# A layer of spectral mixing and expert retrieval on one core: fold sums and turned tiles by DMA, half the tiles negated, small statistics on GpSimd, zero products

## The chip, the cores and the metric

The kernel runs on one core of a Trainium2 chip. The core has a matrix engine (TensorE, PE in the profile, with its weight loads as PEld), a vector engine (VectorE, DVE), an engine for activations (ScalarE, ACT), a general engine (GpSimd, POOL) and a queue engine that mainly starts transfers (SyncE, SP). Each works through its own list of instructions in order, and waits for the others through semaphores. The metric is the time of one execution on the device in microseconds (us); less is better.

## What is computed

The input x has 2048 rows of 512. Its layernorm feeds two branches, whose results are added to x.

```python
a = einsum("bsd,ed->bse", x, dft_hid_re); b = einsum("bsd,ed->bse", x, dft_hid_im)
y = einsum("ts,bse->bte", dft_seq_re, a) - einsum("ts,bse->bte", dft_seq_im, b)
# second branch, 32 heads, 64 x 64 experts
q = einsum("bsd,dhk->bshk", x, w_q)            # halves q1, q2 of 128 each
s1 = q1 . k1, s2 = q2 . k2                     # 64 scores each
# the two best of each, combined, softmax, then rows of u and v:
out = sum over chosen (gate * gelu(x . u[row])) * v[row]
```

The first branch is the real part of a two-dimensional discrete Fourier transform. The second scores each row against two small sets of keys for every head, keeps the best pairs, and mixes rows of two tables.

## The kernel before

The 2048 rows are held as 16 tiles of 128 x 512, in four groups g, each of four tiles q; group order is G = (1, 0, 2, 3). `xn[g]` is a group's tile of 128 x 4 x 512 (x_raw in the profile for group 1, xq for the others). The work has a front, from the start to the first score, and a long rest: the scores (s, line 962; twelve products of 512 columns for each tile and block of heads), interleaved with the products m of the next block, and after them the products with the tables (z, g, v). This change is all in the front. What the front does, group by group:

- **Statistics and norms** (`ln_a`, `ln_b`): BN_STATS and its aggregate for each tile on DVE, a root on ACT, a reciprocal on DVE (line 353) and four small operations (356 to 359), which make `rstd` and `negm`. Then ACT normalises the four tiles in place (371). Where small scratch for BN_STATS is needed, it is taken from the fold's or the statistics' own tiles. A single row, `x5`, is normalised apart (376) and written into group 0's tile later (651).
- **Folds** (`fold_t`, `fold_d`, `fold`): for the first factor (k = 0) the sum of tiles 0, 1 and tiles 2, 3 (407), for the second (k = 1) their difference, 128 x 1024 each, both on DVE; then sums and differences of mirrored columns, with a copy of four columns on GpSimd (399), up to the operand zq (425, 426; v for the last two groups of k = 1).
- **First and second factor** (`main`, 446): for each k and group four f32 products of 512 columns, summed over the groups in four banks of PSUM, p. The row's two products stand apart (`main_row`, 450). `evict` copies the banks out.
- **m** (145, `m_mul`): products of the key matrix with the query weights, which give m, against which tiles are scored. The weights are loaded in four pieces, wq0_0 to wq0_3; the next block's, wq1, are loaded later (131), split into two f16 parts on ACT and GpSimd (155, 160, 163) and used in the m products between scores (141).
- **Turned tiles**: the scores need each tile turned, as two f16 parts (`xt`). For groups 1 and 0 PE turns them (`xpose`: `xpose_a`, 506, four products of a tile with the identity; ACT evicts the upper part, 509; `xpose_b`, 517, subtracts it with `idn`; ACT evicts the lower part, 519). For groups 2 and 3 ACT casts (`upper`, 532), DVE makes the rest (`lower`, 535), and an SP transfer turns both (`cross`, 539).

The program is written in the order of the code; a scheduler then orders each engine's list by its own costs, within dependencies and explicit orders: `pace(i, x)` and `behind(i, x)` put instruction i after x, and `on_dve` returns the DVE instructions of a piece of code. Transfers are queued on the engine that starts them, in its list.

## Time and profile before

| | us |
|---|---|
| median of 3 runs | 1072.82 |
| lowest and highest | 1071.03, 1073.52 |
| profiled execution | 1075.39 |
| its span in the trace | 1073.5 |
| PE busy in the span | 1056.6 |
| DVE busy | 939.7 |
| ACT busy | 732.5 |
| POOL busy | 635.9 |

The span is the time from the first to the last instruction in the trace. A busy share of 98% for PE is an average over all stages; what bounds a stage is read from its waits and its timeline. The clock that PE was granted is part of the page as a row of tenths, one for each fortieth of the span, and of the view by windows with two decimals. The lines that carry the argument are shown with the prediction.

### The profile page before, as it was taken

The page shows a single profiled execution, that of the slowest core. Times are in us where ns is not written, and L with a number is a line of the kernel's source. Part 1 is how long each engine was busy: PE and PEld are TensorE (multiplying, and loading weights), DVE is VectorE, ACT ScalarE, POOL GpSimd, SP SyncE. Part 2 cuts the span into 40 slices and gives each one's busy share as a digit, 9 for nine tenths or more (in the row PEclk, how much of TensorE's full clock was granted, in tenths as well). Part 3 has the DMA queues.
Part 4 walks back from the last instruction along what each step waited for, and adds up shares of the span by engine and source line. Part 5 has one row for each costly group of instructions (what it writes and reads, how often), then busy time and mean ns, then how long its engine had stood idle before and what let it go on. Part 6 is the DMA issues. An engine that isn't in the chain of part 4 may idle for free.

```text
span 1073.5 us, 28588 instructions
## 1 busy us (share of the span) xinstructions
PE 1056.6 (98%) x11101; PEld 698.0 (65%) x11101; DVE 939.7 (88%) x2683; ACT 732.5 (68%) x1367; POOL 635.9 (59%) x610
## 2 busy tenths in 40 slices
PE   6999999999999999999999999999999999999998
PEld 4444555444444544986876958768586785967867
DVE  7979686888999999988999888998999889989972
ACT  5886667859879677435777668676676775868641
POOL 1154858688888755035666566665477757566520
PEclk9899999999999999999999999999999999999999
DMA  9176466345536331377867677776778867676521
GB/s 357 67 193 201 147 242 204 122 151 179 182 137 217 103 120 66 92 256 218 238 191 228 187 233 215 218 219 213 218 205 239 251 190 217 214 237 192 151 50 53
DMA packets 96500, 198.86 MB, mean 185 GB/s; under 512 B 23744, under 2 KB 39381, under 8 KB 96358
## 3 DMA queue, kind: packets, MB, share of 16 engines
q1 hardware_dynamic: 75160, 124.87, 35.7%
q0 software_dynamic: 20896, 71.84, 23.1%
q8 instruction: 88, 1.44, 0.6%
q14 instruction: 54, 0.44, 0.1%
q10 hardware_dynamic: 302, 0.27, 0.1%
HBM read 176.66 MB, written 17.10 MB: 180 GB/s over the span
## 4 chain that ended last, share of the span: by engine, by line
PE 92%; DVE 3%; POOL 2%; issue 1%; DMA 0%; ACT 0%; SPq 0%; POOLq 0%; ACTq 0%
PE z L1138 28%; PE s L962 27%; PE v L1206 26%; PE g L1175 4%; PE p L446 3%; PE m L141 1%; PE vl L1206 1%; DVE vals L970 1%; POOL u L764 1%; DVE idx L974 1%; DMA x_raw<-in_x_dram 0%; PE hy L546 0%; PE hy L545 0%; POOL cx L918 0%; PE xp L506 0%
## 5 line engine op out<-in xcount | busy, mean ns | idle before, releaser
L962 PE MATMUL s<-m,xq 128*128 128x512 f16 x1536 | 338.1, 379 | 0.7 <-ACT ss L967 0.7
L1138 PE MATMUL z<-xb,u 128*128 128x128 f16 x5376 | 306.8, 219 | 0.0
L1138 PEld LDWEIGHTS <-u 128*128 128x128 f16 x5376 | 301.4, 98 | 2.8
L1206 PE MATMUL v<-v,act 128*128 128x512 f16 (+1 forms) x1344 | 288.1, 373 | 0.0
L1270 POOL TENSOR_TENSOR ov<-ov,ga 128x512 f32<-128x512 f32 x125 | 174.0, 1392 | 173.4 <-ACT ga L1262 116.4
L962 PEld LDWEIGHTS <-xq 128*128 128x128 f16 x1536 | 148.2, 98 | 173.9 <-issue 1.8
L1206 PEld LDWEIGHTS <-act 128*128 128x128 f16 x1440 | 138.6, 98 | 141.5 <-issue 2.2
L1233 POOL DMA_INDIRECT ga<-in_uv_dram,eix x128 | 164.9, 1289 | 41.3 <-POOL ov L1270 36.4
L1162 DVE TENSOR_TENSOR L<-io_lam,cmp 128x2048 f16<-128x2048 f16 x112 | 156.9, 1414 | 34.0 <-PE g L1175 29.4
L970 DVE MAX8 vals<-ss 128x8 f32<-128x64 f32 x1024 | 152.7, 216 | 25.3 <-ACT ss L967 25.3
L1141 ACT ACTIVATE act<-z,scl 128x512 f32<-128x512 f32 x112 | 76.2, 681 | 76.5 <-PE z L1138 69.1
L974 DVE FIND_INDEX8 idx<-vals,ss 128x8 uint16<-128x256 f32 x256 | 107.2, 419 | 0.0
L967 ACT ACTIVATE ss<-s,wsc 128x512 f32<-128x512 f32 x112 | 75.3, 683 | 44.2 <-PE s L962 28.4
L944 ACT ACTIVATE cx<-cx 128x896 f32<-128x896 f32 x64 | 60.5, 946 | 58.8 <-DVE cx L924 32.5
L1262 ACT ACTIVATE ga<-ga,za 128x512 f32<-128x512 f32 x128 | 92.2, 722 | 9.7 <-issue 0.2
L1191 ACT ACTIVATE act<-g 128x1024 f16<-128x1024 f32 x56 | 73.2, 1310 | 28.0 <-DVE g L1186 26.0
L1249 DVE SCALAR_TENSOR_TENSOR ga<-ga,px 128x512 f32<-128x512 f32 x128 | 85.9, 677 | 0.0
L1194 DVE TENSOR_TENSOR act<-g,act 128x1024 f16<-128x1024 f32 x56 | 73.0, 1304 | 11.5 <-ACT act L1191 11.1
L1186 DVE SCALAR_TENSOR_TENSOR g<-act,scl,g 128x1024 f32<-128x1024 f32 x56 | 71.5, 1279 | 4.4 <-ACT act L1141 2.8
L1175 PEld LDWEIGHTS <-L 128*128 128x128 f16 x1792 | 51.9, 96 | 8.5 <-issue 2.3
L163 POOL TENSOR_TENSOR wq<-wq,wh 128x1024 f16<-128x1024 f32 x26 | 55.4, 2134 | 2.6 <-ACT wq L160 2.1
L1175 PE MATMUL g<-R,L 128*128 128x32 f16 x1792 | 54.1, 176 | 1.9 <-issue 1.9
(308 smaller groups left out, 1312.9 us busy)
## 6 DMA issues: line engine op xcount, KB each, us to landing
cx<-in_cb_dram SPq DMA_DIRECT2D x50, 448.0 KB
wq<-in_wq_dram SPq DMA_DIRECT2D x32, 512.0 KB
fit<-in_wq_dram SPq DMA_DIRECT2D x28, 512.0 KB
uv<-in_ut_dram SPq DMA_DIRECT2D x16, 512.0 KB
uv<-in_vn_dram SPq DMA_DIRECT2D x16, 512.0 KB
cx<-in_cb_dram SPq DMA_DIRECT2D x28, 224.0 KB
xt_d<-xq SPq DMA_DIRECT2D x16, 256.0 KB
y<-y_d SPq DMA_DIRECT2D x14, 256.0 KB
```

The source lines that it names most:

```text
L962: mm = nc.tensor.matmul(ps, xt[i][:, l, kd, :], m[:, r, kd, :], start=(n == 0), stop=(n == 3 * KD - 1))
L970: nc.vector.max(vals[:, i, w, :, h], s[:, g, :])
L974: nc.vector.max_index(idx[:, i, w].rearrange("p k h -> p (k h)"), vals[:, i, w, 0:2].rearrange("p k h -> p (k h)"), s[:, w * HC:g + 1, :]. ...
L1138: mm = nc.tensor.matmul(p[:, cc * P:(cc + 1) * P], ug[:, l, c % 2, kd, :], xb[:, r, kd, :], start=(n == 0), stop=(n == 3 * KD - 1))
L1141: GL[mm.ins.name] = nc.scalar.activation(act[:, cg * 4:cg * 4 + 4, :].rearrange("p c n -> p (c n)"), p, AF.Gelu_apprx_tanh, scale=zsc)
L1162: nc.vector.tensor_tensor(L.rearrange("p t (l two) -> p t l two", two=2), io_lam.rearrange("p (l two) -> p l two", two=2).unsqueeze(1).to_ ...
L1175: i = nc.tensor.matmul(p[:, hf, t * NC:(t + 1) * NC], L[:, t, :], R[:, hf * 16 + t, :], start=True, stop=True)
L1206: mm = nc.tensor.matmul(pv[d.start // 256][:, d], w16[:, c, :, l], vg[:, r, c % 2, d], start=(c == 0 and k == 0), stop=(c == NC - 1 and k ...
L1233: nc.gpsimd.indirect_dma_start(out=t, out_offset=None, in_=uv, in_offset=bass.IndirectOffsetOnAxis(ap=eix[:, n].rearrange("p k h -> p (k h ...
L1249: nc.vector.scalar_tensor_tensor(t, t, 1.0, T["x"], op0=ALU.mult, op1=ALU.mult, accum_out=T["z", n][:, s:s + 1])
L1262: nc.scalar.activation(t, t, AF.Copy, scale=z)
L1270: T["a"] = nc.gpsimd.tensor_tensor(o, o, t, op=ALU.add)
```

## The change

All of it is in the front.

1. The tiles q = 2, 3 of every group are normalised with negated factors, so they hold the negated values. The first factor's fold becomes a difference, and what reads those tiles takes the sign into account (`sgn`, two identities `idn`). `nr` holds negm and rstd together, and `off0` takes the place of `not0` for group 0.
2. BN_STATS has its own scratch tile `stx`.
3. For groups 2 and 3 the small operations after the reciprocal go to GpSimd; so do the norms of the row x5 and its later write.
4. The second factor's fold sum is made by transfers: SP copies tiles 0, 1 of groups 0, 2, 3 to new tiles `fb` (512 KB each), and GpSimd's accumulating transfer adds tiles 2, 3 (512 KB). For group 1 the accumulation is in place.
5. Group 0's turned tiles go the way of those of groups 2 and 3, with the space of two weight tiles; the 20 products on PE and eight evictions on ACT go.
6. Zero products (`warm`): 29 before the first m products, 13 after them, and 6 into bank p0_00 before group 0's products.
7. Some orders: the row's products stand within group 3's; h = 1 comes first in the last group of k = 0 and the first of k = 1; three of the four absolute maxima of m come before group 3's norms.

The core of the diff:

```diff
-                st = (FF[0, G[0]][:, 0] if n == 1 else SM[n - 1])[:, 6 * (q % 2):6 * (q % 2) + 6]
+                st = stx[:, 6 * (q % 2):6 * (q % 2) + 6]
...
+        if n > 1:
+            nc.gpsimd.tensor_scalar(vp[:, n - 2, 0], mvs[:, g, :, 1], 1e-5, None, op0=ALU.add)
+            nc.gpsimd.tensor_scalar(vp[:, n - 2, 1], mvs[:, g, :, 0], -1.0, None, op0=ALU.mult)
...
+        end = i
+        nm = da.tile([P, 2, 2], F32, name=f"nm{g}")
+        if n < 2:
+            nc.vector.scalar_tensor_tensor(sm[:, 0], var, 1e-5, sm[:, 1], op0=ALU.add, op1=ALU.mult)
+            nc.vector.scalar_tensor_tensor(sm[:, 2], sm[:, 0], -0.5, sm[:, 1], op0=ALU.mult, op1=ALU.mult)
+            nc.vector.scalar_tensor_tensor(rstd[:, g], sm[:, 2], 1.5, sm[:, 1], op0=ALU.add, op1=ALU.mult)
+            if n == 0:
+                nc.vector.tensor_tensor(nm[:, 0], mvs[:, g, 2:4, 0], rstd[:, g, 2:4], op=ALU.mult)
+                end = nc.vector.tensor_scalar(nm[:, 1], rstd[:, g, 2:4], -1.0, None, op0=ALU.mult)
+            else:
+                nc.vector.scalar_tensor_tensor(negm[:, g], mvs[:, g, :, 0], -1.0, rstd[:, g], op0=ALU.mult, op1=ALU.mult)
+                end = nc.vector.tensor_scalar(nm, nr[:, g, :, 2:4], off0, None, op0=ALU.mult)
+        else:
+            v, m = vp[:, n - 2, 0], vp[:, n - 2, 1]
+            nc.gpsimd.tensor_tensor(sm[:, 0], v, sm[:, 1], op=ALU.mult)
+            nc.gpsimd.tensor_tensor(sm[:, 0], sm[:, 0], sm[:, 1], op=ALU.mult)
+            nc.gpsimd.tensor_scalar(sm[:, 2], sm[:, 0], -0.5, 1.5, op0=ALU.mult, op1=ALU.add)
+            nc.gpsimd.tensor_tensor(rstd[:, g], sm[:, 2], sm[:, 1], op=ALU.mult)
+            nc.gpsimd.tensor_tensor(negm[:, g], m, rstd[:, g], op=ALU.mult)
+            nc.gpsimd.tensor_scalar(nm, nr[:, g, :, 2:4], -1.0, None, op0=ALU.mult)
         for q in (0, 2, 1, 3):
             t = xn[g][:, q]
             b, r = negm[:, g, q:q + 1], rstd[:, g, q:q + 1]
-            if g == 0 and q > 1:
-                b, r = nm0[:, 0, q - 2:q - 1], nm0[:, 1, q - 2:q - 1]
...
-                LN[n] = nc.scalar.activation(x5[:, q], x5[:, q], AF.Identity, bias=negm[0:1, 0, q + 2:q + 3],
-                                             scale=rstd[0:1, 0, q + 2:q + 3])
+                nc.gpsimd.tensor_scalar(x5[:, q], x5[:, q], rstd[0:1, 0, q + 2:q + 3], negm[0:1, 0, q + 2:q + 3],
+                                        op0=ALU.mult, op1=ALU.add)
...
-        op = ALU.subtract if k else ALU.add
+        if k:
+            FF["t"] = FB[g]
+            return after
         t = FF["t"] = da.tile([P, 2, 512], F32, tag="ft", name=f"ft{k}_{g}", bufs=1)
-        i = nc.vector.tensor_tensor(t, xn[g][:, 0:2], xn[g][:, 2:4], op=op)
+        i = nc.vector.tensor_tensor(t, xn[g][:, 0:2], xn[g][:, 2:4], op=ALU.subtract)
...
+    def fold_add(g, after):
+        if g == G[0]:
+            t = FB[g] = xn[g][:, 0:2]
+        else:
+            t = FB[g] = da.tile([P, 2, 512], F32, name=f"fb{g}")
+            nc.sync.dma_start(t, xn[g][:, 0:2])
+        pace(nc.gpsimd.dma_start(t, xn[g][:, 2:4], accum_op=ALU.add), after)
...
-        for h in range(2):
+        for h in (1, 0) if g == G[-1 - 3 * k] else (0, 1):
             r = A[k, g][:, h * 512:(h + 1) * 512]
             l = Q[k][g][:, h ^ k]
             for dt in range(2):
-                nc.tensor.matmul(PP[k][dt][h], l[:, dt * P:(dt + 1) * P], r, start=first, stop=last)
-
-    def main_row():
-        for dt in range(2):
-            nc.tensor.matmul(PP[0][dt][0], s5[:, dt * P:(dt + 1) * P], c5r, start=False, stop=False)
+                if last and (k, h) == (0, 0):
+                    nc.tensor.matmul(PP[0][dt][0], s5[:, dt * P:(dt + 1) * P], c5r, start=False, stop=False)
+                i = nc.tensor.matmul(PP[k][dt][h], l[:, dt * P:(dt + 1) * P], r, start=first, stop=last)
+        return i
...
+    def sgn(i):
+        return -XS if i // 4 > 1 else XS
...
-        n = ORD.index(i) % 8
-        t = TS[i] = uf[4 + n // 2][:, n % 2 * 512:n % 2 * 512 + 512].bitcast(F16).rearrange("p (a d) -> p a d", a=2)
-        pace(nc.scalar.activation(t[:, 0], xn[i % 4][:, i // 4], AF.Copy, scale=XS), LN[3])
+        n = ORD.index(i) - 8
+        s = uf[4 + n // 2] if n >= 0 else MS[0, 0 if n < -2 else 2].rearrange("p h k -> p (h k)")
+        t = TS[i] = s[:, n % 2 * 512:n % 2 * 512 + 512].bitcast(F16).rearrange("p (a d) -> p a d", a=2)
+        pace(nc.scalar.activation(t[:, 0], xn[i % 4][:, i // 4], AF.Copy, scale=sgn(i)), LN[3])
...
+    def warm(n, p, alone, after=None):
+        for _ in range(n):
+            i = nc.tensor.matmul(p, wz[:, 0:P], wz[:, P:], start=alone, stop=alone, skip_group_check=not alone)
+            if after is not None:
+                pace(i, after)
+        return i
...
+    wb = pa("warm")
+    first = warm(29, wb, True)
     for t in range(2):
-        m_mul(0, t, (0, 1))
+        i = m_mul(0, t, range(KD))
+    warm(13, wb, True, i)
...
-                for q in (0, 1):
-                    xpose_a(4 * q + G[0], True, LN[2])
...
+            FF["p2"] = FF["p"]
+            for q in range(4):
+                hi = xpose_a(4 * q + G[0], True, LN[3])
+        if n == 3:
+            fold_row(0, FF["end"])
         main(0, g)
         if n == 0:
-            for t in range(2):
-                m_mul(0, t, (2, 3))
             for t in range(2, 4):
-                m_mul(0, t, range(KD))
+                i = m_mul(0, t, range(KD))
+            warm(6, PP[0][0][0], False, i)
+    fold_add(G[0], FF["p2"])
+    for g in G[1:]:
+        fold_add(g, FF["p"])
+    for q in range(4):
+        xpose_b(4 * q + G[0], True, LN[3])
+    made = nc.cur_bb.bb.instructions
+    first = len(made)
+    at = da.tile([P, 1], F32, name="at")
+    m_rest = m_scale(0, MR, at)
+    behind(next(i for i in made[first:] if i.engine == mybir.EngineType.Activation), hi)
...
+        if n:
+            fold(1, g)
+        if n == 1:
+            fold_row(1, FF["end"])
+            nc.gpsimd.tensor_scalar(xn[0][0:1, 2:4], x5, -1.0, None, op0=ALU.mult)
+            small = on_dve(m_rest)
+            behind(small[0], FF["end"])
+        if n == 2:
+            behind(FF["d"][0], small[0])
+            for i in small[1:]:
+                behind(i, FF["end"])
...
-            nc.scalar.activation(xn[0][0:1, 2:4], x5, AF.Copy)
...
         main(1, g)
-        if n == 1:
-            for i in ORD[4:8]:
-                xpose(i, True)
-    for i in ORD[8:12]:
+    for i in ORD[4:12]:
         lower(i, FF["m"])
+    for i in ORD[4:8]:
+        cross(i)
```

In DVE's list this is the place of group 0's statistics, in the front, after group 1's fold. `mvs` holds the statistics, `sm0` the small ones of group 0, `xq0` and `xq2` are the raw tiles of groups 0 and 2. Before:

```order
L345 BN_STATS fo0_1_235<-xq0_100 128x6 x2
L346 BN_AGGR mvs_76<-fo0_1_235 128x2 x2
L353 RECIPROCAL sm0_289<-sm0_289 128x4
L356 SCALAR_TENSOR_TENSOR sm0_289<-mvs_76,sm0_289 128x4
L357 SCALAR_TENSOR_TENSOR sm0_289<-sm0_289 128x4
L358 SCALAR_TENSOR_TENSOR rstd_77<-sm0_289 128x4
L359 SCALAR_TENSOR_TENSOR negm_78<-mvs_76,rstd_77 128x4
L362 TENSOR_SCALAR nm0_158<-rstd_77,not0_79 128x2
L361 TENSOR_SCALAR nm0_158<-negm_78,not0_79 128x2
L345 BN_STATS sm0_289<-xq2_102 128x6 x2
```

Group 0's chain from the reciprocal to its last small operation stands unbroken, and group 2's BN_STATS follow. In the same place of DVE's list, now:

```order
L449 TENSOR_TENSOR zq_139<-fo0_1_295 128x257
L350 BN_AGGR mvs_76<-stx_159 128x2
L349 BN_STATS stx_159<-xq2_101 128x6
L360 RECIPROCAL sm0_345<-sm0_345 128x4
L350 BN_AGGR mvs_76<-stx_159 128x2
L366 SCALAR_TENSOR_TENSOR sm0_345<-mvs_76,sm0_345 128x4
L349 BN_STATS stx_159<-xq2_101 128x6
L367 SCALAR_TENSOR_TENSOR sm0_345<-sm0_345 128x4
L350 BN_AGGR mvs_76<-stx_159 128x2
L368 SCALAR_TENSOR_TENSOR nr_77<-sm0_345 128x4
L349 BN_STATS stx_159<-xq2_101 128x6
L373 SCALAR_TENSOR_TENSOR nr_77<-mvs_76,nr_77 128x4
```

Group 2's BN_STATS have moved in between group 0's small operations; two of group 0's own (not shown) have moved up into group 1's fold.

In GpSimd's list, where before there was only a copy of four columns for each fold, the following stands from group 3's statistics (`sm3`) on; `fb` are the new tiles of the fold sums, `nr` and `nm3` what group 3's norms read:

```order
L377 TENSOR_TENSOR sm3_413<-vp_158,sm3_413 128x4
L378 TENSOR_TENSOR sm3_413<-sm3_413 128x4
L466 DMA x_raw_149<-x_raw_149 128x1024
L379 TENSOR_SCALAR sm3_413<-sm3_413 128x4
L380 TENSOR_TENSOR nr_77<-sm3_413 128x4
L381 TENSOR_TENSOR nr_77<-vp_158,nr_77 128x4
L382 TENSOR_SCALAR nm3_424<-nr_77 128x4
L419 COPY ff0_3_472<-ft0_3_470 128x4
L419 COPY r5_0_481<-r5_0_481 1x2
L466 DMA fb0_495<-xq0_99 128x1024
L466 DMA fb2_498<-xq2_101 128x1024
L466 DMA fb3_501<-xq3_102 128x1024
```

The accumulating transfer of group 1 is issued in the middle of group 3's small operations, and the other three follow the copy of the row's fold.

In SP's list, this is the place of the second block's weight loads (`wq1`) at the end of the front. Before:

```order
L131 DMA wq1_0_599<-in_wq_dram 128x1024
L131 DMA wq1_1_601<-in_wq_dram 128x1024
L131 DMA wq1_2_603<-in_wq_dram 128x1024
L131 DMA wq1_3_605<-in_wq_dram 128x1024
L539 DMA_TRANSPOSE xq2_102<-u4_117 128x8x128 x2
L539 DMA_TRANSPOSE xq2_102<-u5_118 128x8x128 x2
```

The four loads stand ahead of the first transposes, those of group 2. And now:

```order
L577 DMA_TRANSPOSE xq0_99<-wq0_0_167 128x8x128 x2
L577 DMA_TRANSPOSE xq0_99<-wq0_2_176 128x8x128 x2
L131 DMA wq1_0_648<-in_wq_dram 128x1024
L131 DMA wq1_1_650<-in_wq_dram 128x1024
L131 DMA wq1_2_652<-in_wq_dram 128x1024
L131 DMA wq1_3_654<-in_wq_dram 128x1024
L577 DMA_TRANSPOSE xq2_101<-u4_116 128x8x128 x2
L577 DMA_TRANSPOSE xq2_101<-u5_117 128x8x128 x2
```

Group 0's four transposes have come in ahead of the loads.

84 lines of the change are left out of this document (36 added, 48 removed).

## The prediction

> **What bounds the kernel now.** I read the chain of work that ended last, then the waits of PE, then PE's timeline over the first 62 us, then the same stretch window by window, then the other engines there.
>
> ```profile
> PE 92%; DVE 3%; POOL 2%; issue 1%; DMA 0%; ACT 0%; SPq 0%; POOLq 0%; ACTq 0%
> PE m L145 <- DMA wq<-in_wq_dram: 9.4, 1, 9.4
> PE g L1175 <- issue: 1.9, 4, 0.5
> PE p L446 <- DVE zq L425: 0.8, 1, 0.8
> PE s L962 <- ACT ss L967: 0.7, 1, 0.7
> ```
>
> PE carries 92% of the chain. After its first operands (9.4 us) it waits 0.8 us once in the front and then hardly at all. So what the change does to the time is how far it moves the first score (s, L962); that shift passes to the end almost one to one. The timeline (start, length, engine, line, operation, count) shows what stands before it:
>
> ```profile
> 9.40 7.09 PE L145 MATMUL m<-k_sb,wq 128*128 128x64 f32 x32 [9.40 <-DMA wq<-in_wq_dram]
> 16.28 5.05 PE L446 MATMUL p<-v,zq 128*128 128x512 f32 x8
> 21.16 3.68 PE L145 MATMUL m<-k_sb,wq 128*128 128x64 f32 x32
> 25.64 5.40 PE L446 MATMUL p<-v,zq 128*128 128x512 f32 x8 [0.80 <-DVE zq L425]
> 30.88 1.91 PE L506 MATMUL xp<-ident,x_raw 128*128 128x128 f32 x16
> 33.25 3.59 PE L446 MATMUL p<-v,zq 128*128 128x512 f32 x8
> 36.77 1.98 PE L450 MATMUL p<-u,u 1*128 1x512 f32 x4
> 39.16 5.40 PE L446 MATMUL p<-v,zq 128*128 128x512 f32 x8
> 44.50 5.32 PE L446 MATMUL p<-c,zq 128*128 128x512 f32 x12
> 49.66 1.15 PE L506 MATMUL xp<-ident,xq 128*128 128x128 f32 x9
> 60.84 13.11 PE L962 MATMUL s<-m,xq 128*128 128x512 f16 x60
> ```
>
> The first score starts at 60.84. A row group's four products (8 records) take 3.59 in one row and 5.40 in two others: the clock.
>
> ```profile
> 22.50:25.90 3.40, 2.60 (x22) 2.46 (x22) 3.25 (x13) 3.30 (x10) 0.71 (x1) 1.00 1.04 409
> 25.90:29.30 3.40, 3.40 (x5) 1.36 (x5) 3.26 (x8) 2.93 (x8) 0.00 (x0) 0.50 0.98 387
> 36.80:39.50 2.70, 2.70 (x8) 1.05 (x8) 2.60 (x8) 2.70 (x6) 0.64 (x1) 1.00 0.00 0
> 39.50:43.00 3.50, 3.50 (x5) 1.35 (x4) 3.47 (x9) 2.43 (x6) 0.00 (x0) 0.51 0.00 0
> ```
>
> (Window, then its length, busy time of PE, PEld, DVE, ACT and POOL, granted clock, DMA share, GB/s.) Twice the granted clock is 0.50 for 3.4 us, each time costing about 1.7 us: after a stretch of small products with gaps (2.60 of 3.40 busy), and after one of one-row and f16 products without a gap. The first m products also ran at half pace (7.09 against 3.68 for the same 32), behind waits of other engines.
>
> In 25.64 to 60.84 PE is the chain, but with no reserve: group 3's products start at 39.16, just when its operand comes.
>
> ```profile
> 18.74 0.81 ACT L371 ACTIVATE xq<-xq,negm,rstd 128x512 f32<-128x512 f32 x1 [1.03 <-DVE negm L359]
> 18.88 1.28 DVE L345 BATCH_NORM_STATS2 sm<-xq 128x6 f32<-128x512 f32 x2
> 23.57 0.17 DVE L353 RECIPROCAL sm<-sm 128x4 f32<-128x4 f32 x1
> 25.09 0.81 ACT L371 ACTIVATE xq<-xq,negm,rstd 128x512 f32<-128x512 f32 x1
> 28.78 2.04 ACT L587 ACTIVATE u<-m 128x512 f32<-128x512 f32 x4
> 32.88 2.92 ACT L371 ACTIVATE xq<-xq,negm,rstd 128x512 f32<-128x512 f32 x4
> 41.40 0.71 ACT L193 ACTIVATE m<-u,fo 128x512 f16<-128x512 f32 x1
> 35.83 1.23 DVE L407 TENSOR_TENSOR ft<-xq 128x1024 f32<-128x1024 f32 x1 [1.62 <-ACT xq L371]
> 38.68 0.43 DVE L425 TENSOR_TENSOR zq<-fo 128x257 f32<-128x257 f32 x1
> ```
>
> So a second chain runs through statistics, norms on ACT and folds on DVE: the norms of groups 0, 2 and 3 start at 18.74, 25.09 and 32.88, and group 3's fold waits for ACT. Whatever delays these norms reaches PE.
>
> **The change, part by part.** All times are of the profiled execution, 1075.39 us (span 1073.5 and 1.9 around it), which lies 2.6 above the median of 1072.82; I add the difference to the median.
>
> Zero products. One 128x512 f16 product is 13.11/60 = 0.22 us. The 29 and the 13 stand where PE waits anyway, if they lift the clock by 9.4 and 16.3. Then m takes 3.7 instead of 7.1, and group 1's products 3.45 instead of 5.05. This gains nothing by itself, since group 0's operand still comes from DVE. The six add 1.3: 16.9 + 3.45 + 3.68 + 1.3 = 25.3, before that operand. If the clock is not up, they end at 26.5 to 27.9 and their cover is gone, which costs 0 to 1.
>
> Statistics between the folds. In the new order DVE has two BN_STATS (0.64 each) and aggregates (some 0.15) within group 1's fold, and two more pairs between group 0's reciprocal and its last small statistic. Group 1's operand comes near 16.8; group 0's norms start at about 19.9 instead of 18.74, +1.1. What is saved (two pairs fewer after it) falls in DVE's wait for ACT. Group 0's operand: 26.7 instead of 25.64.
>
> Small statistics on GpSimd. The nearest rows:
>
> ```profile
> L837 POOL TENSOR_TENSOR c<-c,if 128x64 f32<-128x64 f32 x7 | 2.3, 326 | 0.1
> 37.09 0.69 DVE L390 TENSOR_TENSOR ff<-ft 128x508 f32<-128x508 f32 x1
> 37.19 0.64 POOL L399 COPY ff<-ft 128x4 f32<-128x4 f32 x1 [3.52 <-DVE ft L407]
> L1215 POOL DMA_DIRECT2D y<-in_x_dram x14 | 14.3, 1023 | 2.1 <-DVE ok L1422 2.0
> ```
>
> Five operations lead from reciprocal to norm. At the first row's size or a little below, 0.25, they take 1.25; if each waits for a DVE operation as the copy seems to (37.19 + 0.64 ends with 37.09 + 0.69), 5 x 0.67 = 3.4. Before, reciprocal to norm took 25.09 - 23.57 = 1.5. The bounds are therefore -0.3 and +1.9 for each of groups 2 and 3; I take 0.1, nearer to the free size, as DVE runs single-input statistics and short folds there. Group 2: reciprocal at 24.7 + 1.6 gives norms at 26.3 (+1.2, nearly all of it group 0's delay), fold from 29.3, operand 32.7. Group 3: reciprocal at 31.1; within the chain stands one accumulating DMA, whose issue takes 1.02. 31.1 + 1.6 + 1.0 = 33.7. ACT is busy until 33.9 anyway (26.3 + 2.92, a root of 0.3, the four copies' 2.04, and three absolute maxima of 0.71 and a short read each, which now stand ahead of these norms). Norms 33.9 instead of 32.88, four of them 2.92, fold 36.9, then 38.68 - 35.83 = 2.85 and the second half of the operand: 40.5.
>
> The Trainium skill's GPSIMD Engine Reference, section 1. Specifications, says GpSimd shares its SBUF interfaces with VectorE and contends with DVE instructions that have two SBUF inputs. The copy's row agrees; by that rule alone the two chains would each take the 3.4 of the upper bound, and the sum below would be 1.9 to 3.8 higher.
>
> Group 3 and the row products. PE is idle from about 36.3 but for four short products, so I charge one half-rate stretch at the place of the old one: from 40.6 to 43.0, 2.4 us at half rate lose 1.2. The one-row products (1.98) move from a place before 38.7 into group 3's, onto the path. 40.6 + 3.45 + 1.98 + 1.2 = 47.2, against 44.50. They wait for the row's fold, which DVE does after group 3's operand, mixed with the second factor's first fold: some 2.6, a little less than the 2.85 of a whole fold, so at 43.1. At half rate PE gets there at 43.5 and the wait is hidden; at full rate it gets there at 42.3 and waits 0.8.
>
> The Trainium skill, TensorE: Matmul & The Clock Gate, Part 1: The HAM clock gate, says that the rate is half or full by how busy a free-running window of about 3.4 us was. The two stretches have that length; but the second followed one without idle time, so busy time alone does not tell what counts, and the sum uses the rows.
>
> Second factor. Sixteen products at full clock are 4 x 3.45 = 13.8; before they took 60.84 - 44.50 = 16.3, since 16 + 4 turning products stood between. The gain is 2.5. 47.2 + 13.8 = 61.0: **+0.2**. This holds if DVE keeps ahead. It loses four fold sums of 1.22, and waits for the accumulating DMAs instead.
>
> ```profile
> q0 software_dynamic: 20896, 71.84, 23.1%
> ```
>
> 71.84 MB in 23.1% of 1073.5 us is 290 GB/s on that queue, so 512 KB need at least 1.8. Issued at about 42.5, 43.6 and 44.6, they land at 46 to 50 by 1.8 to 5 after the issue. Needed: the first at 48 (its fold takes 2.5 before PE's second group at 50.6), the third at 53.5. Cost 0; their rival is below.
>
> Turned tiles by DMA.
>
> ```profile
> 55.78 1.76 SPq L131 DMA_DIRECT2D wq<-in_wq_dram  x4
> 59.97 6.95 SPq L539 DMA_TRANSPOSE xq<-u  x4
> 67.42 1.14 ACT L155 ACTIVATE wh<-wq,wsc 128x1024 f16<-128x1024 f32 x1
> 69.07 1.14 ACT L160 ACTIVATE wq<-wq,wsc 128x1024 f32<-128x1024 f32 x1
> 70.47 2.14 POOL L163 TENSOR_TENSOR wq<-wq,wh 128x1024 f16<-128x1024 f32 x1
> 73.79 0.22 PE L141 MATMUL m<-sums,wh 128*128 128x64 f16 x2
> ```
>
> Group 0's four transposes take SP's queue for 6.95 from about 60, and their tiles are first scored after four tiles of twelve products of 0.22, at 61 + 10.5 = 71.5, so they are hidden. But the wq1 loads, which stood ahead at 55.78, now come behind them, at 67. Landing 2 to 4 later, then 1.14 + 1.14 + 2.14 = 4.4, gives 73.4 to 75.5. PE needs it at 61.0 + 13.0 = 74.0; before, it was ready at 72.6. Cost 0 to 1.5; I take 0.8. Groups 2 and 3 come later in the same queue, with all further scores ahead as cover.
>
> The rest I cost at nothing. The negated tiles only change factors and signs. The row's two norms and its later write go from ACT to GpSimd, where the queue is idle from 20 to 23 and from 46 to 51; the row's first reader on DVE comes at 40.5. SP's three copies of 512 KB come before 45, when the DMA share is 0.00 to 0.22 in the old windows. The eight evictions of turned tiles on ACT are replaced by four casts, all ahead of the first score's eviction. Past 75 us the order of work on PE is the same. Sum: 0.2 + 0.8 = **+1.0 us**: 1072.82 + 1.0 = 1073.8.
>
> **The rivals.**
>
> A, faster: the delays don't come. The statistics only fill gaps of DVE, five GpSimd operations cost what DVE's did, and the clock stays up. If group 3 starts at 39.2 as before, 39.2 + 3.45 + 1.98 + 13.8 = 58.4, or -2.4, with the 0.3 of the lower bound once more -2.7; with the row's wait of 0.8 and ACT's three absolute maxima still 0.4 in the way (33.3 instead of 32.88) it is -1.2. The middle is -1.9: 1070.9. For it: PE's own work in the front is 2.5 us shorter. Against it: the new order puts statistics ahead of what ACT waits for, ACT's maxima ahead of group 3's norms, and PE has gaps before group 3.
>
> B, slower: the clock is half again in group 0's products. From the rows above, 2.60 busy of 3.40 was too little; now PE has some 2.8 there. Then they end at 32.1, the turning of group 1's tiles at 33.6, and the accumulating DMA into group 1's raw tile, which must wait for that, holds GpSimd's queue with group 3's statistics behind it: norms at 35.3, 1.4 later. With +1.0, 1.4 and up to 1.7 for the row products lowering the clock once more: +2.4 to +4.1, 1076 on the middle. It decides where that turning ends later than about 32.
>
> C, slower: the accumulating DMAs land late. If each takes 5 one after another from 42.5, the third lands at 57.5; DVE has a piece of group 3 ahead of group 2's last operand, so PE waits from 54.1 to 58.1: +4.1, in all +5: 1078. It decides at 53.5. Against it: 290 GB/s.
>
> D, no change: what PE saves (2.5) and what the second chain loses (about 2.5 with the rows on the path) cancel, and m doesn't wait: 1072.8, inside the forecast's own range.
>
> **How the numbers follow.** Forecast with D: 0.50, its own range 1071.8 to 1075.4 (the unknowns -1 to +1.6); A 0.20; B 0.20; C, or a GpSimd chain held throughout, 0.10. The range 1070.0 to 1077.6 takes in A, B and part of C. A difference of 0.2%, 2.1 us, is about what a measurement can tell from none. Faster: half of A and what I don't see of that sign, 0.14. Slower: C, nearly all of B and the upper edge of the forecast, 0.33. Same: 0.53.
>
> **What would show it.** Right: norms of groups 0, 2 and 3 near 19.9, 26.3 and 33.9; group 3's products near 40.6; no turning products between the second factor's; the first score near 61; m of wq1 waiting for GpSimd by under 1.5 us. Wrong: a first score below 59 with clock 1.00 throughout (A); clock 0.50 near 26 to 29 and the first DMA issue of GpSimd waiting for PE (B); PE waiting for zq behind DVE, behind a DMA, past 50 (C).

## The result, and the profile after

The changed kernel takes **1078.13 us** (median of 5 runs, 1077.4 to 1078.77), the kernel before 1071.17 beside it (5 runs, 1071.02 to 1073.52). The ratio is 1.0058, with a 95% interval of 1.0044 to 1.0073: slower by 0.58%, some 6.2 us. The forecast was 1073.8 with a range up to 1077.6; its likeliest case was a change too small to measure. The time came out just above the range, on the side to which it gave 0.33.

The page of the profiled execution (1078.55 us, so 0.4 above the median), its span and the chain that ended last:

```profile
span 1076.7 us, 28680 instructions
PE 90%; DVE 4%; POOL 3%; ACT 1%; issue 1%; DMA 0%; SPq 0%; POOLq 0%; ACTq 0%
```

PE is still the chain, with two points less, which DVE and POOL took over. The waits of PE say where (line and releaser, us in total, times, longest):

```profile
PE p L481 <- DVE zq L448: 2.3, 3, 1.1
PE xp L554 <- ACT xq L545: 1.6, 1, 1.6
PE p L481 <- DVE zq L449: 1.3, 1, 1.3
PE m L141 <- POOL wq L164: 1.3, 1, 1.3
```

The 9.4 us of waiting for the first weights are gone but for 1.3 ahead of the first zero product and 0.3 behind the last, since the zero products fill them. The waits ahead of groups 1, 0 and 2 are the first row, two waits ahead of group 3 the second and third. The last, at the first product of `m` of wq1, lies on the path for certain. PE's timeline through the front:

```profile
16.51 3.70 PE L481 MATMUL p<-v,zq 128*128 128x512 f32 x8 [0.61 <-DVE zq L448]
26.13 3.70 PE L481 MATMUL p<-v,zq 128*128 128x512 f32 x8 [1.11 <-DVE zq L448]
32.55 3.70 PE L481 MATMUL p<-v,zq 128*128 128x512 f32 x8 [0.54 <-DVE zq L448]
41.05 3.36 PE L481 MATMUL p<-v,zq 128*128 128x512 f32 x4 [1.34 <-DVE zq L449]
44.34 1.39 PE L480 MATMUL p<-u,u 1*128 1x512 f32 x2
45.66 1.13 PE L481 MATMUL p<-v,zq 128*128 128x512 f32 x2
46.72 1.12 PE L480 MATMUL p<-u,u 1*128 1x512 f32 x2
47.77 1.55 PE L481 MATMUL p<-v,zq 128*128 128x512 f32 x2
49.11 8.34 PE L481 MATMUL p<-c,zq 128*128 128x512 f32 x16
57.29 7.03 PE L481 MATMUL p<-c,v 128*128 128x512 f32 x16
64.16 13.11 PE L1017 MATMUL s<-m,xq 128*128 128x512 f16 x60
78.66 0.20 PE L141 MATMUL m<-sums,wq 128*128 128x64 f16 x1 [1.32 <-POOL wq L164]
```

Groups 1, 0 and 2 (16.51, 26.13, 32.55) run at full rate, 3.70 for eight records. Group 3 starts at 41.05, and its eight records with the four of the row's products take 8.06 until the second factor starts at 49.11. Its first four records run at half rate (3.36), and so does the beginning of the second factor (8.34 for 16 records, then 7.03 for 16). The first score starts at 64.16. The windows show the clock (columns as before):

```profile
38.10:41.50 3.40, 1.74 (x5) 0.49 (x4) 3.33 (x9) 3.40 (x8) 0.71 (x1) 1.00 0.78 271
41.50:44.90 3.40, 3.40 (x5) 1.17 (x4) 2.92 (x10) 2.51 (x6) 3.23 (x4) 0.50 0.40 77
44.90:48.30 3.40, 3.40 (x7) 0.89 (x6) 1.39 (x2) 2.94 (x8) 1.33 (x1) 1.00 1.04 193
48.30:51.80 3.50, 3.50 (x6) 1.42 (x5) 3.47 (x12) 2.29 (x5) 1.93 (x1) 0.51 0.98 187
```

There are two half-rate stretches in which PE is busy throughout, each losing half of 3.4: 3.4 us in all. One follows a window with little PE work (1.74 of 3.40), the other a window that is full, but more than half of it with one-row products (1.92). The window ahead of the first, 34.7 to 38.1, had as little PE work (1.76), and the clock behind it was full.

The chain that ends in the wait for `m` begins on GpSimd (timelines of GpSimd, DVE, ACT and SP):

```profile
46.97 3.26 POOL L697 TENSOR_SCALAR xq<-x 1x1024 f32<-1x1024 f32 x1 [2.10 <-DMA fb<-xq]
56.60 0.39 POOL L115 PARTITION_ALL_REDUCE pw<-mx  x1 [6.36 <-issue]
57.02 0.17 DVE L116 TENSOR_SCALAR pw<-pw 128x3 f32<-128x3 f32 x1 [3.46 <-POOL pw L115]
57.88 2.56 ACT L222 ACTIVATE m<-u,msc 128x512 f16<-128x512 f32 x4 [3.35 <-DVE wsc L208]
63.75 5.57 SPq L577 DMA_TRANSPOSE xq<-wq  x4
69.38 2.00 SPq L131 DMA_DIRECT2D wq<-in_wq_dram  x4
73.39 1.15 ACT L156 ACTIVATE wh<-wq,wsc 128x1024 f16<-128x1024 f32 x1 [0.57 <-DMA wq<-in_wq_dram]
76.46 2.13 POOL L164 TENSOR_TENSOR wq<-wq,wh 128x1024 f16<-128x1024 f32 x1
```

The row's later write takes GpSimd 3.26 us and ends at 50.23. The all-reduce behind it in the same queue starts only at 56.60. DVE and ACT stand for it (3.46 and 3.35), the halves of `m` and then the lower halves of the turned tiles come later, the transposes start at 63.75, the wq1 loads behind them at 69.38, and the last of it reaches PE at 78.66, 1.32 late.

### The profile page after: what moved, and what is told of

Same layout as the page of the kernel before. It is cut to its first block, busy times and chain, and to the rows that moved or that the text cites. A ratio compares the mean times of both kernels' runs of the same rounds, so it can differ in the third digit from the quotient of the medians.

```text
span 1076.7 us, 28680 instructions
## 1 busy us (share of the span) xinstructions
PE 1061.3 (99%) x11129; PEld 696.4 (65%) x11129; DVE 937.7 (87%) x2676; ACT 729.2 (68%) x1360; POOL 648.9 (60%) x635
## 4 chain that ended last, share of the span: by engine, by line
PE 90%; DVE 4%; POOL 3%; ACT 1%; issue 1%; DMA 0%; SPq 0%; POOLq 0%; ACTq 0%
PE z L1193 28%; PE v L1261 26%; PE s L1017 26%; PE g L1230 4%; PE p L481 2%; PE m L141 2%; PE vl L1261 1%; ACT xq L391 1%; DVE vals L1025 1%; POOL wq L164 1%; POOL u L819 1%; DVE idx L1029 1%; DMA x_raw<-in_x_dram 0%; DVE ft L429 0%; POOL u L495 0%
## 5 line engine op out<-in xcount | busy, mean ns | idle before, releaser
L1325 POOL TENSOR_TENSOR ov<-ov,ga 128x512 f32<-128x512 f32 x125 | 176.7, 1413 | 170.7 <-ACT ga L1317 111.7
```

The costliest lines, as they stand in the source:

```text
L1325: T["a"] = nc.gpsimd.tensor_tensor(o, o, t, op=ALU.add)
```

## The experiments

The theory after this reading: three things on the path. The row's products within group 3, with an operand that comes later; the half-rate stretches that they and PE's wait ahead of group 3 bring; and the row's write on GpSimd, which delays the all-reduce. The rivals: that the stretches fall by chance, whatever the order is; that idle PE alone brings them; that the zero products are what harms; and that the small statistics on GpSimd hold group 3.

The runs come from several chips, on which the kernel before has medians from 1068.9 to 1072.6; so each ratio is against the runs of before on its own chip, and kernels are compared with each other first within one chip (the first, the second and third, and the one without zero products; then the four of both edits, front order, zero products alone and filler; then the changed kernel again, the replaced row and all orders).

**The kernel of before once more**, unchanged, as a base for the traces.

> The kernel before, unchanged, for a second trace. Theory 1 (the half-rate stretches of the clock depend on what PE does in the front): two of them again before the first score, near 26 and 40 us, the first score at 60.8 within 0.3, and none near 480, since the old trace's third one there stands by itself. Theory 2 (where the stretches fall is chance, so that the two traces compared differ by luck): their number or place in the front differs from the first trace, and the first score moves by 1.7 us for each.

1071.9 us (10 runs, 1069.02 to 1073.84) against 1071.19: ratio 1.0003 [0.9993, 1.0014]. Its trace, however, isn't the one that the prediction used:

```profile
25.80 3.65 PE L446 MATMUL p<-v,zq 128*128 128x512 f32 x8
38.39 3.60 PE L446 MATMUL p<-v,zq 128*128 128x512 f32 x8
58.59 13.11 PE L962 MATMUL s<-m,xq 128*128 128x512 f16 x60
```

Groups 0 and 3 run at full rate (3.65 and 3.60, where the first trace of before had 5.40 twice), and the first score starts at 58.59 instead of 60.84. The same program has two half-rate stretches in its front in one execution and none in another (between 21 us, where the clock's record begins here, and the first score). That accounts for 2.25 us. The execution that the prediction was worked out against was one with both. Against this one the changed kernel's first score is 5.57 later, and with the 1.32 at `m` it is 6.89 behind. Instruction by instruction that offset stays, 6.85 at 250 us; a second trace of the changed kernel (below) has 7.07 there. Past 476 us, where the work passes from the scores to the next stage, the profiled executions lose between nothing and 4 us, whatever the kernel: the before kernel 4.2 in its first trace and none in this one, the changed kernel 2.5 in its first trace and none in its second. This doesn't belong to the change.

**The row's products early**: the row's fold and products back ahead of group 3, as before.

```diff
-                if last and (k, h) == (0, 0):
-                    nc.tensor.matmul(PP[0][dt][0], s5[:, dt * P:(dt + 1) * P], c5r, start=False, stop=False)
...
+        if n == 3:
+            fold_row(0, FF["end"])
+            main_row()
...
-        if n == 3:
-            fold_row(0, FF["end"])
```

> The changed kernel with the row's fold and the row's two one-row products back ahead of group 3's fold and products, as in the kernel before. Theory 1 (the one-row products cost 2 us because they moved onto the path, where PE had waited idle before group 3): group 3's products start at 41.1 as in the changed kernel and end by 46.5 instead of 49.1, the first score comes at 61.5 to 62.2 instead of 64.2, and the time falls by 2 to 2.7 us. Theory 2 (the row products only fill a place that the second factor's operands need anyway): the second factor then waits for DVE behind the accumulating transfer (which landed at 46.9 in the changed kernel's trace), and the first score moves by less than 0.8.

1076.56 us (1073.71 to 1078.87): ratio 1.0045 [1.0028, 1.0062]. In the trace the clock stays full through the front, group 3's products take 3.70 from 41.12, and the second factor starts at 44.66 instead of 49.11. Yet the first score comes at 60.61, only 3.55 earlier, and PE waits longer at `m`:

```profile
PE m L141 <- POOL wq L164: 2.4, 1, 2.4
PE p L479 <- DVE v L448: 1.6, 1, 1.6
```

With the products early, the all-reduce is what ends last: it starts at 53.78, 6.01 after GpSimd's write. DVE stands 2.83 for it with the last fold behind, and PE 1.6 for that fold and 2.4 at `m`: 4.0 us, which the changed kernel pays only in part since it is late anyway.

**The row's write on ScalarE**, alone.

```diff
-            nc.gpsimd.tensor_scalar(xn[0][0:1, 2:4], x5, -1.0, None, op0=ALU.mult)
+            nc.scalar.activation(xn[0][0:1, 2:4], x5, AF.Copy, scale=-1.0)
```

> The changed kernel with the late write of the single row (1 x 1024) on ACT, with the factor -1, instead of GpSimd. Theory 1 (GpSimd's library for the all-reduce of m's maximum could be loaded early in the kernel before; now its loading stands behind the row's write, 6.4 us without anything that the profile shows, and the halves of m, the lower parts, the transposes and the wq1 loads all come late by it): the all-reduce ends near 51 instead of 57, the four transposes start near 60 instead of 63.8, and the wait of 1.3 us at the first m product of wq1 is gone: time -1.3, first score unchanged at 64.2. Theory 2 (wq1 is late only because its loads stand behind the transposes in SP's list): the wait stays at over 0.8.

1077.77 us (4 runs, 1074.61 to 1081.08): ratio 1.0071 [1.0043, 1.01], which doesn't part it from the changed kernel (1.0058 on another chip) or the kernel with the row early. The trace does: the all-reduce starts at 50.99, the transposes at 60.12 instead of 63.75, and PE doesn't wait at `m`; the offset against the second trace of before is 5.54 at 250 us, and was 6.85. The first score stays at 64.33 with its two stretches. So the chain from the write to `m` is as described. Alone it is worth about the 1.3 us of that wait, which the spread of these four runs hides. That spread goes with the clock: two runs (1074.61 and 1075.13) had a mean granted clock of 0.996, the other two (1080.42 and 1081.08) 0.991.

**Both together.** The two diffs above in one kernel.

> The changed kernel with two parts undone together: the row's products ahead of group 3 and the row's late write on ACT. Theory 1 (the loss consists of the row on the path, of half-rate stretches that follow idle time in front of group 3, and of the library load behind the row's write): PE no longer waits 1.6 before the second factor's last group nor 2.4 at m, the first score comes at 59.0 to 59.4 (60.6 - 1.55), no stretch before it, and the time is 1069.5 to 1071, within 0.2% of the kernel before. Theory 2 (the transfers of the fold sums bound the second factor): PE waits over 1 us for DVE within it, and the first score stays above 60.

1074.18 us (12 runs, 1071.26 to 1075.16) against 1072.59: ratio 1.0012 [1.0, 1.0023]. On the same chip a kernel with the changed order and a filler (below) took 1078.3. Two edits give back most of the loss, 0.41% between those two (1.0053 to 1.0012), where each alone gave little that can be told apart. The timeline of PE:

```profile
36.05 1.98 PE L484 MATMUL p<-u,u 1*128 1x512 f32 x4
40.67 5.11 PE L479 MATMUL p<-v,zq 128*128 128x512 f32 x8 [1.01 <-DVE zq L448]
45.62 7.03 PE L479 MATMUL p<-c,zq 128*128 128x512 f32 x16
59.35 13.11 PE L1020 MATMUL s<-m,xq 128*128 128x512 f16 x60
```

The row's products stand in PE's wait for group 3, one half-rate stretch (40.13 to 43.54) is left, and the second factor runs in 13.73 without a wait. The first score is where the first theory put it (59.35). What is left there beside the before kernel at full clock (58.59) is that stretch and an operand 2.3 later, minus the turning products. Behind it come two waits at `m` that the theory didn't have, 0.92 at 73.44 and 0.77 at 83.56: with an earlier first score, `m` waits again although the write is off GpSimd.

**The front's order put right further**: on top of this, group 2's BN_STATS behind group 0's small statistics, the first accumulating DMA behind group 3's, and the absolute maxima behind group 3's norms.

```diff
+            i = nc.scalar.activation(m[:, 0, kd, :], pm[kd], AF.Abs, scale=1.0 if at is None else at,
+                                     accum_out=mx[:, kd:kd + 1])
+            if at is not None:
+                pace(i, LN[3])
...
+            i = nc.vector.bn_stats(st, xn[g][:, q])
+            if n == 2 and q == m:
+                pace(i, FF["s1"])
...
-    fold_add(G[0], FF["p2"])
+    fold_add(G[0], FF["s3"])
```

> As the kernel with the row ahead of group 3 and its write on ACT, and three orders more: group 2's BN_STATS wait for the end of group 0's small statistics, the accumulating transfer of group 1 is issued behind group 3's small statistics on GpSimd, and the absolute maxima of m come behind group 3's norms on ACT. Theory 1 (what group 3 lost, 41.1 against 38.4 without stretches, is the sum of these three orders: 0.6, 1.0 and what ACT is busy ahead of it): group 3's norms start at 32.3 to 33 instead of 34.4, its products at 39.0 to 39.8, the first score at 57 to 58, and the time is 1 to 2 us below the kernel before. Theory 2 (the small statistics on GpSimd themselves are the loss): the norms still start at 33.8 or later and the first score stays above 58.5.

1072.95 us (12 runs, 1070.75 to 1074.87): ratio 1.0006 [0.9994, 1.0019]. Group 0's products start at 24.68 instead of 26.0, group 3's at 39.18 instead of 40.67, so these three orders are worth 1.5 us at group 3. Its norms start at 32.33 (34.42 in the changed kernel, 31.85 in the second trace of before) with the small statistics still on GpSimd, so those are not what held group 3 by more than some 0.5. The first score gains only 0.2 (59.13): the 16 products of the second factor now wait 0.59 for an eviction and the half-rate stretch falls on group 3 again. The time can't be told from that of the kernel before; the first theory's 1 to 2 us below it did not come.

**The zero products.** Left out of the changed kernel (its `warm` calls and the clearing of their operand removed), and put alone into the kernel of before:

```diff
-    first = warm(29, wb, True)
...
-    warm(13, wb, True, i)
...
-            warm(6, PP[0][0][0], False, i)
```

> The changed kernel without any zero product. Theory 1 (the zero products keep the clock up for group 0's products, worth some 1.7 us there, and through the turning of group 1's tiles they also release GpSimd's queue earlier): a half-rate stretch comes back near 26, group 0's products take 5 instead of 3.7, the accumulating transfer of group 1 is issued 1 to 2 us later, and the first score comes 1 to 2 us later than 64.2. Theory 2 (the clock in group 0 doesn't matter, since PE waits for DVE before groups 2 and 3 anyway): the first score stays within 0.4. Theory 3 (the zero products only shift the stretches into group 3): the first score comes earlier, by up to 3.

> The kernel before with nothing of the change but the zero products (29, 13 and 6) and m's first products in one piece. Theory 1 (they hold the clock, and that alone is worth what the stretches cost the kernel before: 2.2 us in its first trace, 60.84 against 58.59 without them): first score at 58.3 to 59 in the trace, no stretch before it, and the median falls from 1071.2 towards the 1069 to 1070 of the runs at clock 1.00; the spread shrinks. Theory 2 (group 0's operand sets the pace, and the zero products only stand in the way): the first score later than 59, time the same or up to 1.3 longer.

Without them the changed kernel takes 1082.2 us (1080.89 to 1084.12), ratio 1.0108 [1.0091, 1.0125]. The changed kernel has 1.0058 in its first comparison and 1.0093 [1.0077, 1.011] in a second one (below), so the difference is 0.50% or 0.15%, and the second pair of intervals overlaps. In the trace the clock is half from 39.08 to 56.15, 17 us in one piece, and the first score comes at 68.18, 4.0 later. The mean granted clock is 0.990 to 0.993 in all four runs; the changed kernel has 0.996 or 0.997 in seven of its ten and 0.991 to 0.993 in the other three. Group 0's products run at full rate (3.65) all the same. In the kernel of before the zero products change nothing: 1071.2 us, ratio 0.9993 [0.9982, 1.0004], first score at 59.00. So they aren't what harms. That they help the changed kernel is likely but not shown, and it would be at another place than the one that the prediction spoke of.

**A filler ahead of group 3**: seven more zero products in PE's wait there, against the theory that PE's idle time brings the stretch.

```diff
             fold_row(0, FF["end"])
-        main(0, g)
+            warm(7, PP[0][0][0], False, last)
+        last = main(0, g)
```

> The changed kernel with seven more zero products (1.5 us) into bank p0_00 between group 2's products and the four products that finish group 1's turned tiles, where PE sat idle (36.2 to 37.9). Theory 1 (the two half-rate stretches at 41.5 and 48.3 follow the idle time before group 3, and cost 1.7 and 1.3 us): the stretch at 41.5 goes, group 3's products and the row's take 5.6 instead of 8.1, and the first score comes 1.7 to 3 earlier than 64.2; the time falls by as much. Theory 2 (the stretches come from the one-row products themselves, which hardly load PE): at least one stretch stays, after the row's products, and the first score comes at most 1.7 earlier. Theory 3 (chance): no change on the average of the runs.

1078.3 us (4 runs, 1077.06 to 1081.91): ratio 1.0053 [1.0037, 1.0069], nothing gained. In the trace the clock is half for even longer, 41.82 to 55.47, though PE is busy there without a gap. This is the longest of the four executions (1081.91, clock 0.993); the others had 0.996 to 0.998, so such a long stretch is not in each. The filler took one wait of 1.6 us; the 1.34 right ahead of group 3 stayed.

**The row's products replaced by nine zero products** of 128 rows, with about the same length. The row's part is left out.

```diff
-                    nc.tensor.matmul(PP[0][dt][0], s5[:, dt * P:(dt + 1) * P], c5r, start=False, stop=False)
+                    warm(5 - dt, PP[0][dt][0], False, i)
```

> The changed kernel with the row's two one-row f32 products (1.98 us) in group 3's place replaced by nine zero products on all 128 rows (5 and 4, 1.97 us); the row's part of the first factor is left out of the result. Theory 1 (one-row products count little for the clock): at most one half-rate stretch, at the start of group 3's products after the idle time, none after it; the first score at 61 to 62.6, and the time 1.5 to 3 below the changed kernel on the same chip. Theory 2 (only idle time counts): the same stretches as the changed kernel, the first score at 63.5 to 65 and the time within 1 us of it.

The changed kernel itself ran again beside it, on another chip than in the first comparison:

> The changed kernel, unchanged, on the chip of the two kernels beside it. Theory 1 (the row's one-row products within group 3's products leave windows in which the array does little, and PE is idle ahead of them, so at least one half-rate stretch follows in nearly every execution): first score again at 62.5 to 66, one to four stretches between 40 and 56, wait for wq1 at the first m product 1 to 1.5, time 1077 to 1079. Theory 2 (the two stretches of the first trace were chance): the first score near 61.1 and the time below 1075.

The changed kernel took 1079.45 us there (1076.2 to 1081.59), ratio 1.0093 [1.0077, 1.011]; with the products replaced 1076.4 (1075.1 to 1078.27), ratio 1.0068 [1.0052, 1.0083]. The traces don't part them: half rate at 40.76 and at 47.59 in the one, two windows in a row (40.40 to 47.22) in the other, 6.8 us in both, waits at `m` of 1.71 and 1.76, and first scores at 63.99 and 63.37, between the two theories. The medians lie 3 us apart, the intervals overlap a little. The granted clock, which is on record for every run, says more: 0.991 to 0.997 in the changed kernel's five (mean 0.994), 0.995 to 0.998 with the products replaced (mean 0.997), 0.997 to 1.00 in the before kernel's nine on this chip (mean 0.999). By these means the clock takes some 6.5, 3.2 and 1.2 us of the span (an estimate: what is missing to 1, times the span), and the first two differ by as much as the medians. So the stretches don't fall by chance whatever the order is: none of the changed kernel's ten runs is above 0.997, and seven of before's nine are. The one-row products probably add to them, but the stretch at group 3's start comes without them too.

**All orders at once**: the front's order and both edits, the small statistics back on DVE, and the wq1 loads issued by GpSimd instead of SP. The wish was a kernel that beats both.

```diff
-            MS[j, "w"] = nc.sync.dma_start(MS[j, t], wq[j, t // 2, t % 2])
+            MS[j, "w"] = (nc.gpsimd if j == 1 else nc.sync).dma_start(MS[j, t], wq[j, t // 2, t % 2])
...
-        if n > 1:
-            nc.gpsimd.tensor_scalar(vp[:, n - 2, 0], mvs[:, g, :, 1], 1e-5, None, op0=ALU.add)
-            nc.gpsimd.tensor_scalar(vp[:, n - 2, 1], mvs[:, g, :, 0], -1.0, None, op0=ALU.mult)
...
-        if n < 2:
+        if True:
```

> The changed kernel with: the row's products ahead of group 3, the row's late write on ACT, the small statistics of groups 2 and 3 on DVE again, group 2's BN_STATS behind group 0's small statistics, the absolute maxima of m behind group 3's norms, and the loads of wq1 issued by GpSimd, which is idle then, instead of SP behind the transposes. Kept of the change: fold sums and group 0's turned tiles by transfers, the negated tiles, the zero products. Theory 1 (these are the parts that gain, 2.5 us of turning products, once nothing in front of group 3 is late): group 3's products start at 38.2 to 39, the first score at 55.8 to 57.2, no wait at m over 0.5, and the time is 1.5 to 3 us below the kernel before. Theory 2 (the transfers then become the bound): PE waits for DVE within the second factor, behind a transfer, by 1 to 3, and the first score stays at 58 or later; or the transposes come too late for group 0's first score, with a wait there.

1075.99 us (1074.67 to 1077.11): ratio 1.0057 [1.0044, 1.0071]. That is 3.5 less than the changed kernel on the same chip (1.0093), but no kernel that beats the one before. Group 3's norms came 2.5 earlier (31.87 instead of 34.42), and DVE then stood still, in its timeline:

```profile
40.03 0.16 DVE L418 TENSOR_TENSOR fo<-x_raw 128x2 f32<-128x2 f32 x1 [3.17 <-DMA x_raw<-x_raw]
```

This is a piece of the second factor's fold of group 1, which reads the accumulating transfer and stands in DVE's list ahead of group 3's operand. The transfer, issued at 31.78, could be read at 40.03. In the changed kernel DVE is late anyway and this is hidden; as soon as the rest is early, it holds group 3 (41.38), and half rate falls on it (38.99 to 45.82; first score 61.76). Later PE waits 1.76 at `m` (85.86), where the first theory had no wait over 0.5, and 1.71 for ACT (103.84).

**That fold behind**, with three more moves: `m` of wq1 two tiles later, and the f16 upper halves of the turned tiles behind the halves of `m` on ScalarE.

```diff
+    end = FF["end"]
     fold(1, G[0])
+    for i in FF["d"]:
+        behind(i, end)
...
-        if n:
-            for i in ORD[4 * n:4 * n + 4]:
-                upper(i)
         main(1, g)
+    for i in ORD[4:16]:
+        upper(i)
...
-        MST0 = MST if safe else {4: 1, 6: 2, 7: 3, 8: 4, 9: 5, 10: 6}
+        MST0 = MST if safe else {6: 1, 7: 2, 8: 3, 9: 4, 10: 5, 11: 6}
```

> The kernel before it (all orders: row's products and fold early, row's write on ScalarE, small statistics back on DVE, BN_STATS and absolute maxima behind what others wait for, wq1 loads issued by GpSimd), with four more moves: the second factor's pieces of group 1 stand behind group 3's operand in DVE's list, the products of m of wq1 come two tiles later, the f16 upper halves of the turned tiles are cast behind m's own halves on ScalarE. Theory 1 (what held group 3 back was only the accumulating transfer of group 1, 3.2 us in DVE's list): DVE no longer waits for a transfer ahead of group 3's operand, group 3's products start at 38 to 39, the first score at 57 to 59.5 (one half-rate stretch), no wait at m; the time is 1 to 3 us under that of the kernel of before, ratio 0.997 to 0.999. Theory 2 (the front is bound by something else that comes up in its place: the transfers again, now in the second factor, or m's halves or the turned tiles' casts ahead of the first scores): first score at 60 or later, or waits of over 1.5 us within the first tiles, ratio 1.002 to 1.006.

1084.99 us (1084.57 to 1085.95): ratio 1.0148 [1.0134, 1.0162], the slowest of all. Its PE, and the two rows that hold it:

```profile
38.70 3.60 PE L480 MATMUL p<-v,zq 128*128 128x512 f32 x8
50.45 7.03 PE L480 MATMUL p<-c,v 128*128 128x512 f32 x16
60.62 19.90 PE L1023 MATMUL s<-m,xq 128*128 128x512 f16 x84 [3.14 <-ACT u L518]
103.31 3.57 PE L732 MATMUL p<-u,one 128*1 128x512 f32 x4 [4.44 <-DVE usc L799]
...
55.84 4.25 ACT L573 ACTIVATE u<-xq 128x512 f16<-128x512 f32 x8
101.48 0.37 POOL L115 PARTITION_ALL_REDUCE uvpFalse<-asums  x1 [5.99 <-ACT ss L1028]
```

Both theories held in part. The front is what the first one said: no wait ahead of group 3 (38.70), no half-rate stretch from 6 to 60 us, and the last product of the second factor ends at 57.5. That is 6.7 before the changed kernel's first score and 1.1 before that of the last before trace. With fold sums and turned tiles by DMA and the zero products still in it, the front can be as short as before; the loss there came with the order, with the row's write on GpSimd, and with the half-rate stretches behind them. (The small statistics are back on DVE in this kernel, its norms of group 3 start at 32.18; with them on GpSimd, in the kernel with the front's order, it was 32.33. Moved alone they weren't tried.) Then two of my own moves cost more than this. The casts now stand on ScalarE ahead of the second factor's evictions, and the first score waits 3.14 for those. At 103 PE waits 4.44 for a small DVE operation behind a second all-reduce, which again starts 6 us after GpSimd's work before it, and the clock is half from 101.5 to 111.7. That the moved steps of `m` bring PE to this wait is inferred; it wasn't tried alone.

## Why the forecast was too small, point by point

**The base: failed.** The prediction took its durations from one execution of before and added the difference to the median. That execution had two half-rate stretches in the front (its own rows of 0.50 and 0.51), which moved its first score to 60.84; the next one had none and 58.59. "61.0: +0.2" should have read +2.4. The page had the hint: the profiled execution lay 2.6 above the median of the timed ones. (Not every timed execution of before is at full clock either, 0.996 to 1.00 in the ten runs above, so against the median this step is worth somewhat less than 2.25.)

**The clock: mis-sized.** "I charge one half-rate stretch at the place of the old one ... lose 1.2." Two came, 3.4 us in all. The rival for it (B) named the one-row products as a second cause, "up to 1.7"; that part came. Its trigger, group 0's products at half rate, didn't: 3.70 at 26.13, and GpSimd's first issue waited only 0.32 for PE.

**Group 3 and the row: nearly right.** Its products were put at 40.6 and came at 41.05; the row's products took the path as charged, and some 0.5 more, since at full clock a pair of them and a pair of group 3's now follow each other at 1.05 each (45.66, 46.72, 47.77).

These add up to the first score: 0.45 + (3.4 - 1.2) + 0.5 = 3.15, against 64.16 - 61.0 = 3.16.

**The row's write at nothing: failed.** "The row's two norms and its later write go from ACT to GpSimd, where the queue is idle." The queue was idle, but what stood behind it was the all-reduce. The write waits for a transfer until 46.97, takes 3.26, and the all-reduce starts 6.36 after it. The wait at `m` was forecast (0.8, by the loads behind the transposes) and measured 1.32; the loads came at 69.38 rather than 67 because of this chain, and without the write on GpSimd the wait is gone as long as the first score stays late (64.33). With the first score at 59.35 it was 0.92, so the 0.8 for the loads has its place too.

Together: the forecast's 1.0, the base's 2.25, the first score's 3.16 and 0.52 at `m` make 6.93; the trace has 6.89 between the changed kernel and the before kernel at full clock.

**Right in the number, for group 3 not in the path:** the norms, forecast at 19.9, 26.3 and 33.9:

```profile
19.37 0.81 ACT L391 ACTIVATE xq<-xq,nr 128x512 f32<-128x512 f32 x1 [2.10 <-DVE nr L373]
25.85 0.28 POOL L381 TENSOR_TENSOR nr<-vp,nr 128x4 f32<-128x4 f32 x1
26.16 0.81 ACT L391 ACTIVATE xq<-xq,nr 128x512 f32<-128x512 f32 x1 [1.81 <-POOL nr L381]
31.40 0.35 POOL L377 TENSOR_TENSOR sm<-vp,sm 128x4 f32<-128x4 f32 x1 [0.19 <-DVE sm L360]
32.40 1.18 POOL L466 DMA_DIRECT2D x_raw<-x_raw  x1 [0.32 <-PE xp L542]
33.32 0.51 POOL L379 TENSOR_SCALAR sm<-sm 128x4 f32<-128x4 f32 x1
34.19 0.20 POOL L381 TENSOR_TENSOR nr<-vp,nr 128x4 f32<-128x4 f32 x1
34.42 0.81 ACT L391 ACTIVATE xq<-xq,nr 128x512 f32<-128x512 f32 x1 [1.02 <-POOL nr L381]
```

The prediction let ACT set group 3's norms (33.9) and GpSimd's chain end just ahead of it (33.7). It was the other way round: ACT was free at 33.4 and waited 1.02 for GpSimd. The two charges lay close together, so the number came out nearly right all the same. GpSimd's small operations took 0.20 to 0.35 (0.51 behind the DMA's issue), the free size, and the issue within group 3's chain 1.18 where 1.02 was charged. The Trainium skill's GPSIMD Engine Reference, section 1. Specifications, speaks of contention with DVE instructions that have two SBUF inputs; the trace agrees, at a small price: the operation of line 381 took 0.28 for group 2, beside a two-input operation of DVE, and 0.20 for group 3, with DVE idle. The upper bound, 0.67 for each, did not come. The second factor without turning products takes 49.11 to 64.16, 15.05; less 1.35 for the 2.7 us of it at half rate this is 13.7, and 13.8 was forecast. The fold sums by DMA cost the changed kernel nothing (rival C did not come: no product of the second factor waits for DVE). The landing was mis-sized all the same: against "1.8 to 5 after the issue" the first of the three came 4.7 behind (issued at 42.18, read at 46.91), and in the last two kernels the transfers took 7.1 to 9.1. One of the runs above shows how near that bound lies.

**Open** stays what sets the clock. In all traces the front's stretches last 3.41 us or a whole multiple of it (6.83, 13.65, 17.07). The Trainium skill, TensorE: Matmul & The Clock Gate, Part 1: The HAM clock gate, has free-running windows of about 3.4 us; these lengths and the same program with two stretches or none agree with that. What counts within a window isn't settled. Busy time alone gives no rule: the changed kernel has 2.30 of 3.41 busy from 24.45 to 27.86 and full clock behind it, 1.77 from 34.69 to 38.10 and full clock, 1.76 from 38.10 to 41.52 and half. Counting the one-row products as idle gives none either: the before kernel has them for 1.98 us of a window that is otherwise full in both of its traces (36.15 to 39.56, and 34.87 to 38.28), and the clock behind it is half in the first and full in the second. What can be said is that a window with little PE work (1.5 to 1.8 of 3.41), or one with the row's products in it, stands ahead of each stretch in the changed kernel's two traces, and that the one kernel with most of the change and no wait ahead of group 3 (the last one) has none up to 60 us.

## What to carry to other kernels

Before a trace serves as the base of a sum, see whether its execution is a typical one: where its time lies above the median, look for what this execution alone has, here half-rate stretches of 2.25 us, more than the effect forecast. Where the granted clock is on record for every run, compare it between kernels before calling a stretch chance. A small operation that moves to an idle queue is priced by what stands behind it in that queue, not by its length. And two edits that each hide behind the other are tried together: alone they gave little that could be told apart, together most of the loss.
